# Top-k attention and a two-layer MLP on one core: the second MLP layer as seven block products, with block sums on GpSimd

## The chip, the cores and the metric

The kernel runs on one core of a Trainium2 chip. The metric is the time of one execution on the device, in microseconds (us); lower is better. The time before the change is 1482.96 us, the median of three runs (1481.1 to 1486.69). Engines are named as in the profile: PE is TensorE (matmuls), PEld its weight loads, DVE VectorE, ACT ScalarE, POOL GpSimd, SP the engine that issues most DMAs.

## The reference, cut to what matters

```
scores = (q @ k^T) / sqrt(64)                  # 8 batches x 8 heads, 576 x 576 each
kth    = the 32nd largest score of each row
attn   = softmax of scores, those below kth left out
x      = (attn @ v), heads side by side        # 4608 tokens x 512
h      = x @ w_in                              # 512 x 2048
g      = max(0.01 * h, h)
out    = g @ w_out                             # 2048 x 512
```

All of it is fp32 at the kernel's edges except the weights, which come as 64-bit floats and are rounded on the chip in the first 60 us.

## The kernel before, in words

**Attention.** The work on scores is cut into 144 units of 128 rows for two heads at a time. One step of the main loop starts one unit on DVE and carries the units before it on, so that four or five are in flight: in step s, DVE finds the 32 largest of each row of unit s (`top_k`, L299 to L318: two TENSOR_TENSORs at L306 that sort the halves of a row pairwise, then rounds of MAX8 and MATCH_REPLACE8), POOL makes the bias of unit s-1 (`nbias`, L327 and L328), ACT masks it, takes exponents with their sum and scales it by the reciprocal (`rz`, L344, on DVE; scaling at L347). In the next step POOL splits unit s-2 into two halves (`split`, L356), SP writes these to DRAM and reads them back transposed (L357, L359) into `wT`; two steps later PE weighs the values with it (L398, L410) into `x`, the tokens' input to the MLP. At the end of every even step PE makes the scores of two units (L235) and ACT copies them to SBUF (L242).

**MLP.** Tokens are taken in chunks: two of 128, then seventeen of 256 (`CHUNKS`, L54). For a chunk of 256, the first layer makes the hidden values transposed: for each of 16 blocks of 128 hidden units, four matmuls of 256 columns into `ph` (L467), and after two blocks a Prelu by ACT into `gT` (L473). The second layer takes the 256 tokens as two row tiles; each accumulates 16 matmuls of 512 columns into `pz` (L479), which ACT copies to `o_sb` (L488) and sends to the output by a DMA from its own queue (L489). `ph` and `pz` take turns in two PSUM buffers. The chunks of 128 have a first layer of their own (`hidden_of_few`, L429).

**Order.** The order of the work is written out by hand; nothing reorders it. `mlp` (L455) is a generator that yields the columns of its matmuls as a cost after every few of them. At seven places in a step the main loop calls `mlp_steps(budget)` (L501), which runs it for so many columns; `slot_budget` (L548) spreads the columns that are waiting evenly until the next chunk is due. What is left at the end runs through in one go (L702). Each engine works through its own instructions in order.

**Loads.** Queries and keys of the 32 pairs of heads come by `load_qk` (L162) into five buffers of their own and, for three pairs in eight, into the three `raw` buffers that held the weights at the start; `load_more` (L575, from L592 on for q and k) decides at the end of a step what is loaded next, `load_waiting` (L184) issues one load from a list at the start of a step.

Of the kernel before, what the change touches and what calls it, by code (L numbers as in the profile page):

```python
# [20 lines left out]
def kernel(  # L21
# [23 lines left out]
    HP = DMODEL // P  # L45
# [4 lines left out]
    NFC = DFF // P  # L50
    WCH = 1024
# [2 lines left out]
    CHUNKS = [128] * 2 + [256] * 17  # L54
    assert sum(CHUNKS) == B * S
    CHMAX = max(CHUNKS)
    LOADED, LOADED_V = 5, 5

    const = ctx.enter_context(tc.tile_pool(name="const", bufs=1))
    xpool = ctx.enter_context(tc.tile_pool(name="xpool", bufs=2))  # L60
    loads = ctx.enter_context(tc.tile_pool(name="loads", bufs=LOADED))
    raws = ctx.enter_context(tc.tile_pool(name="raws", bufs=3))
    work = ctx.enter_context(tc.tile_pool(name="work", bufs=2))
# [19 lines left out]
    gT = const.tile([P, NFC, CHMAX], F32, name="gT")  # L83
# [76 lines left out]
    qk_of, v_of = {}, {}  # L160

    def load_qk(pi, at_once=True):  # L162
        if pi % (LOADED + 3) < LOADED:
            qt = loads.tile([P, S], F32, name="qt")
            kt = loads.tile([P, S], F32, name="kt")
        else:
            raw = raws.tile([P, WCH, 4], U16, name="raw").rearrange("p n w -> p (n w)").bitcast(F32)
            qt, kt = raw[:, 0:S], raw[:, S:2 * S]
        waiting.extend([(qt, qT[pi]), (kt, kT[pi])])
        qk_of[pi] = qt, kt  # L170
        if at_once:
            while waiting:
                nc.sync.dma_start(*waiting.pop(0))
# [255 lines left out]
    def hidden_of_few(ch, x):  # L429

        g_of = {}
        for j in range(NFC // 4):
            ph = ps_ml.tile([P, 512], F32, name="ph", tag="ml")
            for c in range(HP):
                nc.tensor.matmul(ph, x[c][:, 0:P], w_in[c][:, j * 512:(j + 1) * 512],  # L435
                                 start=(c == 0), stop=(c == HP - 1))
                if c == 1:
                    yield 2 * 512
            g_of[j] = raws.tile([P, 2 * DMODEL], U16, name="scale", bufs=2).bitcast(F32)
            nc.scalar.activation(g_of[j], ph, AF.Prelu, alpha=SLOPE)  # L440
            yield 2 * 512
            if j:
                yield from turned(j - 1, g_of)
        few[ch] = g_of
# [3 lines left out]
    def turned(j, g_of):  # L448
# [3 lines left out]
        nc.scalar.copy(gT[:, 4 * j:4 * (j + 1), 0:P], pt)  # L452
        yield 2 * P

    def mlp(ch):  # L455

        n = CHUNKS[ch]
        t0 = sum(CHUNKS[:ch])
        x = x_of[ch]
        if ch < EARLY:  # L460
            yield from hidden_of_few(ch, x)
        for f0 in range(0, NFC if ch >= EARLY else 0, 2):
            ph = ps_ml.tile([P, 2, CHMAX], F32, name="ph", tag="ml")
            for i in range(2):
                f = f0 + i
                for c in range(HP):
                    nc.tensor.matmul(  # L467
                        ph[:, i, 0:n], w_in[c][:, f * P:(f + 1) * P], x[c][:, 0:n],
                        start=(c == 0), stop=(c == HP - 1),
                    )  # L470
                    if c == 1 or i == 0 and c == HP - 1:
                        yield 2 * max(n, 225)
            nc.scalar.activation(gT[:, f0:f0 + 2, 0:n], ph[:, :, 0:n], AF.Prelu, alpha=SLOPE)  # L473
            yield 2 * max(n, 225)
        for r0 in range(0, n, P):
            m = min(P, n - r0)
            pz = ps_ml.tile([P, 512], F32, name="pz", tag="ml")
            for f in range(NFC):
                nc.tensor.matmul(  # L479
                    pz[0:m, 0:DMODEL], gT[:, f, r0:r0 + m], w_out[f // 4][:, f % 4, :],  # L480
                    start=(f == 0), stop=(f == NFC - 1),
                )
# [4 lines left out]
            o_sb = work.tile([P, DMODEL], F32, name="o_sb", bufs=1)  # L487
            nc.scalar.copy(o_sb[0:m], pz[0:m, 0:DMODEL])  # L488
            nc.scalar.dma_start(out[t0 + r0:t0 + r0 + m, :], o_sb[0:m])  # L489
# [11 lines left out]
    def mlp_steps(budget):  # L501
        owed[0] += budget
        while owed[0] > 0:
            if running[0] is None:
                if not ready:
                    owed[0] = 0.0
                    return
                running[0] = mlp(ready.pop(0))
            cost = next(running[0], None)
            if cost is None:  # L510
                running[0] = None
            else:
                owed[0] -= cost
                backlog[0] -= cost
# [44 lines left out]
    with tc.manual_schedule():  # L559
# [15 lines left out]
        def load_more(s):  # L575

            at_once = 2
            while len(v_of) < NPAIR:
                n = len(v_of)
                due = values_at(starts[n])[0]  # L580
                if n < LOADED_V:
                    load_v(n)
                elif values_at(last[n - LOADED_V])[0] > s:
                    break
                elif due > s + 2:
                    load_v(n, at_once=False)
                elif at_once:
                    load_v(n)
                    at_once -= 1
                else:  # L590
                    break
            while len(qk_of) < NPAIR:  # L592
                n = len(qk_of)
                if n < LOADED or not to_keep and n < LOADED + 3:
                    load_qk(n)
                elif not to_keep and last[n - LOADED - 3] + 8 <= s and not waiting:
                    load_qk(n, at_once=False)
                else:
                    break

# [36 lines left out]
        def keep(weighed, *place):  # L637
            for u, po in weighed:
                keep_values(u.pairs[0], po, u.b, u.q0)
            attended(*place)  # L640

        for s in range(len(steps) + LAG + 1):
            assert s < 7 or not to_keep
            cur, old, older, new = unit(s), unit(s - 1), unit(s - 2), ()
            in_haste = s - 2 in HASTY
            if s % 2 == 0:
                new = [u for u in steps[s + 2:s + 4] if u]
            if new and new[0] in early_units:
# [24 lines left out]
            if old:  # L673
                exponents(old, 0)
            weighed = values(s, MIDDLE)
            if old:
                exponents(old, 1)
                sums(old)
            keep(weighed, s, MIDDLE)
            mlp_steps(budget)  # L680
            slot()
            if s % 2:
                slot()
            if old:
                reciprocals(old)
            mlp_steps(budget)
            if old:
                normalize(old, 0)
                normalize(old, 1)
            mlp_steps(budget)  # L690
            slot()
            slot()
            if unit(s + 3) in early_units:
                fetch_scores(unit(s + 3))
            mlp_steps(budget)
            if new:
# [5 lines left out]
        mlp_steps(1e9)  # L702


_OUT = ((4608, 512), "float32")
# [56 lines left out]
```

## Time and profile before

| what | us |
|---|---|
| median of three runs | 1482.96 |
| the profiled execution | 1484.13 |
| its span in the trace | 1482.3 |
| PE busy | 1421.1 (96%) |
| DVE busy | 1313.7 (89%) |
| ACT busy | 1035.8 (70%) |
| POOL busy | 504.6 (34%) |
| second layer, L479 | 513.7 busy on PE, 1152 records |
| first layer, L467 | 491.0 busy on PE, 2176 records |

The chain of work that ended last runs 84% through PE, 7% through DVE and 5% through ACT. An fp32 matmul of the code leaves two records each of weight load and matmul, so 1152 records are 576 matmuls. Matmul records overlap each other: a group's busy time divided by its count is shorter than the mean duration of one record. The page cuts the span into 40 slices and gives the busy share of each in tenths. Rows of groups give the line, engine, operation, output and inputs with their shapes and the count, then busy us and mean ns of one, then the idle time before them and what ended it.

### The profile page before, as it was taken

To read this page: it belongs to the slowest core of one execution; us is meant where nothing else is said; L and a number is where in the kernel's file an instruction comes from. 1 tells how busy PE (TensorE), PEld (TensorE's weight loads), DVE (VectorE), ACT (ScalarE), POOL (GpSimd) and SP (SyncE) were. 2 spreads that over 40 slices of the span, in tenths; PEclk is the share of its full clock that TensorE was granted. 3 is DMA by queue.
4 is the path that set the end of the run, shared out by engine and by line. 5 is a ranking of instruction groups with operands and counts; after the bars stand their busy time and mean duration, and the time that the engine had idled before them with its cause. 6 is when DMAs were issued, how large, how long until landed. Compare 5 with 4: busy or idle time off the path is not lost.

```text
span 1482.3 us, 25928 instructions
## 1 busy us (share of the span) xinstructions
PE 1421.1 (96%) x9032; PEld 906.0 (61%) x9034; DVE 1313.7 (89%) x3401; ACT 1035.8 (70%) x2148; POOL 504.6 (34%) x580
## 2 busy tenths in 40 slices
PE   7859989899999999999999999999999999999999
PEld 2335447557575757575766666766666666666674
DVE  7987899899999999999999999999999999999700
ACT  8877777667676767676777777767677777777610
POOL 3211242333433333343333333333433333333400
PEclk9988998999999999999999999999999999999999
DMA  8932152666666654676565655666666555544510
GB/s 335 335 121 96 58 146 68 179 178 167 181 164 174 161 142 129 177 197 186 161 178 161 174 129 142 180 191 176 175 165 173 160 142 129 165 131 140 137 44 15
DMA packets 379252, 232.06 MB, mean 157 GB/s; under 512 B 320368, under 2 KB 321905, under 8 KB 377201
## 3 DMA queue, kind: packets, MB, share of 16 engines
q1 hardware_dynamic: 373936, 220.97, 52.6%
q10 hardware_dynamic: 5184, 9.44, 1.7%
q8 instruction: 71, 1.16, 0.3%
q14 instruction: 61, 0.49, 0.1%
HBM read 55.77 MB, written 95.55 MB: 102 GB/s over the span
## 4 chain that ended last, share of the span: by engine, by line
PE 84%; DVE 7%; ACT 5%; DMA 2%; issue 1%; POOL 1%; SPq 0%; ACTq 0%; DVEq 0%; POOLq 0%
PE pz L479 32%; PE ph L467 31%; PE wide L398 10%; PE wide L235 5%; PE narrow L235 3%; DVE tops L311 2%; DVE pairs L316 1%; PE wide L410 1%; PE ph L435 1%; ACT s_sb L242 1%; ACT s_sb L335 1%; DMA raw<-in_weights_dram 1%; ACT s_sb L332 1%; DVE w_out L156 1%; ACT s_sb L347 1%
## 5 line engine op out<-in xcount | busy, mean ns | idle before, releaser
L311 DVE MAX8 tops<-pairs 128x8 f32<-128x288 f32 (+1 forms) x1152 | 639.0, 596 | 0.0
L479 PE MATMUL pz<-w_out,gT 128*128 128x512 f32 x1152 | 513.7, 599 | 0.5 <-ACT scale L440 0.5
L467 PE MATMUL ph<-x,w_in 128*128 128x256 f32 x2176 | 491.0, 383 | 0.0
L316 DVE MATCH_REPLACE8 pairs<-tops,pairs 128x288 f32<-128x288 f32 (+1 forms) x864 | 461.9, 542 | 0.0
L467 PEld LDWEIGHTS ph<-x,w_in 128*128 128x128 f32 x2176 | 407.8, 190 | 82.3 <-issue 29.6
L327 POOL TENSOR_TENSOR nbias<-tops 128x2 f32<-128x2 f32 x144 | 108.2, 751 | 849.7 <-DVE tops L311 842.3
L479 PEld LDWEIGHTS pz<-w_out,gT 128*128 128x128 f32 x1152 | 215.4, 191 | 258.2 <-issue 255.9
L356 POOL COPY split<-s_sb 128x1152 uint16<-128x1152 uint16 x268 | 298.8, 1142 | 5.1 <-ACT s_sb L347 5.1
L347 ACT ACTIVATE s_sb<-s_sb,rz 128x576 f32<-128x576 f32 x288 | 207.1, 769 | 33.7 <-DVE rz L344 33.3
L335 ACT ACTIVATE s_sb<-s_sb,nbias 128x576 f32<-128x576 f32 x288 | 218.8, 761 | 0.0
L332 ACT ACTIVATE s_sb<-s_sb,nleast 128x576 f32<-128x576 f32 x288 | 208.0, 768 | 4.7
L306 DVE TENSOR_TENSOR pairs<-s_sb 128x576 f32<-128x576 f32 x288 | 205.4, 754 | 4.9
L398 PE MATMUL wide<-wT,vt 128*64 128x128 f32 (+1 forms) x2560 | 158.0, 287 | 12.3 <-ACT wT L375 8.4
L398 PEld LDWEIGHTS wide<-wT,vt 128*64 128x64 f32 (+1 forms) x2560 | 129.4, 140 | 59.2 <-issue 37.7
L242 ACT COPY s_sb<-wide 128x704 f32<-128x704 f32 x130 | 98.4, 757 | 58.1 <-PE wide L235 58.1
L473 ACT ACTIVATE gT<-ph 128x512 f32<-128x512 f32 x136 | 80.5, 592 | 81.5 <-PE ph L467 81.3
L422 ACT COPY x<-wide 128x128 f32<-128x128 f32 (+1 forms) x160 | 32.2, 260 | 136.7 <-PE wide L398 117.5
L488 ACT COPY o_sb<-pz 128x512 f32<-128x512 f32 x36 | 21.1, 587 | 99.1 <-PE pz L479 99.1
L328 POOL TENSOR_SCALAR nbias<-nbias 128x2 f32<-128x2 f32 x144 | 85.8, 596 | 12.6
L344 DVE RECIPROCAL rz<-ze 128x2 f32<-128x2 f32 x144 | 22.4, 156 | 71.7 <-ACT ze L340 71.6
L235 PE MATMUL wide<-kt,qt 64*64 64x352 f32 x704 | 72.8, 473 | 3.8 <-ACT wT L375 3.1
L316 DVE MATCH_VALUE_LOAD pairs<-tops,pairs 128x8 f32 x864 | 65.8, 76 | 0.0
(70 smaller groups left out, 773.3 us busy)
## 6 DMA issues: line engine op xcount, KB each, us to landing
apart<-split SPq DMA_DIRECT2D x268, 288.0 KB, 2.1
raw<-in_weights_dram SPq DMA_DIRECT2D x15, 1024.0 KB, 6.9
vt<-in_vk_dram SPq DMA_DIRECT2D x32, 320.0 KB, 3.5
out_dram<-o_sb ACTq DMA_DIRECT2D x36, 256.0 KB, 2.7
kept<-gT SPq DMA_DIRECT2D x12, 576.0 KB, 3.0
s_sb<-kept SPq DMA_DIRECT2D x12, 576.0 KB, 4.2
qt<-in_qT_dram SPq DMA_DIRECT2D x20, 288.0 KB, 3.5
kt<-in_kT_dram SPq DMA_DIRECT2D x20, 288.0 KB, 3.2
```

The lines of the kernel that those rows point to most:

```text
L235: nc.tensor.matmul(to[r0:r0 + LEFT, i, :], qt[d, q0:q0 + LEFT], kt[d, k0:k1], start=True, stop=True)
L242: nc.scalar.copy(u.both[:, :, k0:k1], to)
L306: nc.vector.tensor_tensor(pairs[:, :, n, :], u.both[:, :, 0:HS], u.both[:, :, HS:S], op)
L311: nc.vector.max(out=u.tops[:, i, r, :], in_=rest[i])
L316: nc.vector.match_replace(out=rest[i], in_to_replace=u.tops[:, i, r, :], in_values=rest[i], imm_value=LOWEST)
L332: nc.scalar.activation(u.s[i], u.s[i], AF.Prelu, bias=u.nleast[:, i:i + 1], scale=1.0, alpha=BELOW)
L335: nc.scalar.activation(u.s[i], u.s[i], AF.Exp, bias=u.nbias[:, i:i + 1], scale=SCALE, accum_out=u.z[:, i:i + 1])
L347: nc.scalar.activation(u.s[i], u.s[i], AF.Copy, bias=0.0, scale=u.rz[:, i:i + 1])
L356: nc.gpsimd.tensor_copy(split, pairs[:, :, h])
L398: nc.tensor.matmul(po[n * D:(n + 1) * D, side, 0:P], v_of[u.pairs[0]][k, at, side, :], u.wT[k, at + side * NKC if at + 1 < NKC else at, :] ...
L467: nc.tensor.matmul(ph[:, i, 0:n], w_in[c][:, f * P:(f + 1) * P], x[c][:, 0:n], start=(c == 0), stop=(c == HP - 1),)
L479: nc.tensor.matmul(pz[0:m, 0:DMODEL], gT[:, f, r0:r0 + m], w_out[f // 4][:, f % 4, :], start=(f == 0), stop=(f == NFC - 1),)
```

## The change

The second layer of the chunks of 256 tokens is done in seven block products in place of eight. The hidden values of a chunk are seen as a 2 x 2 matrix of blocks (two row tiles of 128 tokens, two halves of the 2048 hidden units), `w_out` as 2 x 2 blocks (two halves of the hidden units, two halves of the 512 outputs). Each product is eight matmuls of 256 columns. It needs sums of blocks:

- of the weights, once: `t1`, `t2`, `t4` in the three `raw` buffers, given to POOL from step 7 on, and one block of `w_out` overwritten by a difference when the first chunk of 256 begins;
- of the hidden values, in each chunk: `s1`, `s2`, and two blocks of `gT` overwritten; eight sums of 128 x 512;
- of the products: three sums of 128 x 256 in SBUF. Two partial sums are carried by accumulation in PSUM. ACT copies PSUM out seven times a chunk, 128 x 256 each.

The sums are all POOL's. `sum_later` puts them on a list, `sum_now(3)` issues up to three in the middle of every step, and `sum_now()` the rest at two places in `mlp` where a product is about to need them. The output DMAs of these chunks leave from SP at the start of the next step (`send_now`), four of 128 KB a chunk. The first layer pairs block f0 with block f0 + 8, so that both halves of the hidden values grow together.

Since the `raw` buffers now hold the weights' sums, queries and keys have seven buffers of their own, and their loads are ordered by another condition.

```diff
-    LOADED, LOADED_V = 5, 5
+    LOADED, LOADED_V = 7, 5
...
-        if pi % (LOADED + 3) < LOADED:
-            qt = loads.tile([P, S], F32, name="qt")
-            kt = loads.tile([P, S], F32, name="kt")
-        else:
-            raw = raws.tile([P, WCH, 4], U16, name="raw").rearrange("p n w -> p (n w)").bitcast(F32)
-            qt, kt = raw[:, 0:S], raw[:, S:2 * S]
+        qt = loads.tile([P, S], F32, name="qt")
+        kt = loads.tile([P, S], F32, name="kt")
...
+    def sum_now(count=1000):
+        for to, a, b, op, then in later[:count]:
+            nc.gpsimd.tensor_tensor(to, a, b, op)
+            if then is not None:
+                to_send.append(then)
+        del later[:count]
+
+    def send_now():
+        while to_send:
+            nc.sync.dma_start(*to_send.pop(0))
...
+            sum_later(t1, w_block(0, 1, g), w_block(0, 0, g), ALU.subtract)
+            sum_later(t2, w_block(1, 1, g), t1, ALU.subtract)
+            sum_later(t4, w_block(1, 0, g), t2, ALU.subtract)
...
+            sum_later(w_block(0, 1, g), w_block(1, 1, g), w_block(0, 1, g), ALU.subtract)
...
-            nc.scalar.activation(gT[:, f0:f0 + 2, 0:n], ph[:, :, 0:n], AF.Prelu, alpha=SLOPE)
-            yield 2 * max(n, 225)
+            nc.scalar.activation(halves_of_g[:, :, f0, :], ph, AF.Prelu, alpha=SLOPE)
+            if f0 % 4 == 3:
+                at = slice(f0 - 3, f0 + 1)
+                sum_later(s1[:, at, :], g21[:, at, :], g22[:, at, :], ALU.add)
+                sum_later(s2[:, at, :], s1[:, at, :], g11[:, at, :], ALU.subtract)
+                sum_later(g21[:, at, :], g11[:, at, :], g21[:, at, :], ALU.subtract)
+            yield 2 * n
+
+        def product(to, g, w, first=False):
+            for f in range(HALF):
+                nc.tensor.matmul(to, g[:, f, :], w(f), start=(first and f == 0), stop=(f == HALF - 1),
+                                 skip_group_check=not first)
+                if f % 4 == 3:
+                    yield 4 * COLS
+
+        def keep_sum(ps):
+            part = work.tile([P, COLS], F32, name="o_sb", bufs=6)
+            nc.scalar.copy(part, ps)
+            return part
+
+        def add(part, other, r, j):
+            sum_later(part, part, other, ALU.add, (place(r, j), part))
...
+        pa = ps_ml.tile([P, 512], F32, name="pz", tag="ml")
+        pb = ps_ml.tile([P, 512], F32, name="pz", tag="ml")
+        px, py, pz = pa[:, 0:COLS], pb[:, 0:COLS], pb[:, COLS:2 * COLS]
+        yield from product(px, g11, lambda f: w_at(f, 0), first=True)
+        p1 = keep_sum(px)
+        yield from product(py, g12, lambda f: w_at(f + HALF, 0), first=True)
+        p2 = keep_sum(py)
+        sum_now()
+        for f0 in (0, 4):
+            at = slice(f0, f0 + 4)
+            sum_later(g12[:, at, :], g12[:, at, :], s2[:, at, :], ALU.subtract)
+        yield from product(px, s2, of("t2"))
+        u2 = keep_sum(px)
+        add(p1, p2, 0, 0)
+        yield from product(pz, s1, of("t1"), first=True)
+        p5 = keep_sum(pz)
+        yield from product(px, g21, lambda f: w_at(f, 1))
+        u3 = keep_sum(px)
+        sum_now()
+        yield from product(pz, g12, lambda f: w_at(f + HALF, 1))
+        p35 = keep_sum(pz)
+        add(u3, p5, 1, 1)
+        yield from product(px, g22, of("t4"))
+        c21 = keep_sum(px)
+        add(u2, p35, 0, 1)
+        to_send.append((place(1, 0), c21))
+        yield 0
...
-        return NFC * HP * max(n, 225) + -(-n // P) * NFC * DMODEL
+        return NFC * HP * n + 7 * HALF * COLS
...
-                if n < LOADED or not to_keep and n < LOADED + 3:
+                if n < LOADED:
                     load_qk(n)
-                elif not to_keep and last[n - LOADED - 3] + 8 <= s and not waiting:
-                    load_qk(n, at_once=False)
+                elif last[n - LOADED] // 2 * 2 - 1 <= s and (not waiting or starts[n] <= s + 5):
+                    load_qk(n, at_once=starts[n] <= s + 5)
...
             load_waiting()
+            send_now()
...
             keep(weighed, s, MIDDLE)
+            if s == 7:
+                sum_weights()
+            sum_now(3)
             mlp_steps(budget)
```

The chunks of 128 keep their second layer; only their output leaves in two halves of 256 columns. After the last step, what is left on the two lists is issued.

More of the change, by code (lines that the diff above doesn't have):

```diff
@@ L453, in turned, with w_at, w_block, sum_later @@
         yield 2 * P
+    HALF, COLS = NFC // 2, DMODEL // 2
+    summed = {}
+    def w_at(f, j):
+        return w_out[f // 4][:, f % 4, j * COLS:(j + 1) * COLS]
+    def w_block(i, j, g):
+        return w_out[2 * i + g][:, :, j * COLS:(j + 1) * COLS]
+    later, to_send = [], []
+    def sum_later(to, a, b, op, then=None):
+        later.append((to, a, b, op, then))
+    def sum_now(count=1000):
[7 more added lines that the diff above has]
+            nc.sync.dma_start(*to_send.pop(0))
+    def sum_weights():
+        for name in ("t1", "t2", "t4"):
+            t = raws.tile([P, WCH, 4], U16, name="raw").rearrange("p n w -> p (n w)").bitcast(F32)
+            summed[name] = t.rearrange("p (f n) -> p f n", n=COLS)
+        for g in range(2):
+            t1, t2, t4 = [summed[name][:, 4 * g:4 * (g + 1), :] for name in ("t1", "t2", "t4")]
+            sum_later(t1, w_block(0, 1, g), w_block(0, 0, g), ALU.subtract)
+            sum_later(t2, w_block(1, 1, g), t1, ALU.subtract)
+            sum_later(t4, w_block(1, 0, g), t2, ALU.subtract)
+    def sum_last_weights():
+        for g in range(2):
+            sum_later(w_block(0, 1, g), w_block(1, 1, g), w_block(0, 1, g), ALU.subtract)
     def mlp(ch):
@@ L460, in mlp @@
         if ch < EARLY:
-            yield from hidden_of_few(ch, x)
-        for f0 in range(0, NFC if ch >= EARLY else 0, 2):
+            yield from plain(ch, n, t0, x)
+            return
+        if ch == EARLY:
+            sum_last_weights()
+        halves_of_g = gT.rearrange("p (h f) n -> p h f n", h=2)
+        (g11, g21), (g12, g22) = [[halves_of_g[:, h, :, r * P:(r + 1) * P] for r in range(2)] for h in range(2)]
+        s1 = raws.tile([P, HALF, P], F32, name="top", bufs=2)
+        s2 = raws.tile([P, HALF, P], F32, name="top", bufs=2)
+        for f0 in range(HALF):
             ph = ps_ml.tile([P, 2, CHMAX], F32, name="ph", tag="ml")
             for i in range(2):
-                f = f0 + i
+                f = f0 + i * HALF
                 for c in range(HP):
@@ L471, in mlp @@
                     if c == 1 or i == 0 and c == HP - 1:
-                        yield 2 * max(n, 225)
-            nc.scalar.activation(gT[:, f0:f0 + 2, 0:n], ph[:, :, 0:n], AF.Prelu, alpha=SLOPE)
-            yield 2 * max(n, 225)
+                        yield 2 * n
[5 more added lines that the diff above has]
+                sum_later(g21[:, at, :], g11[:, at, :], g21[:, at, :], ALU.subtract)
@@ new lines, in mlp @@
+            yield 2 * n
+        def product(to, g, w, first=False):
[10 more added lines that the diff above has]
+            sum_later(part, part, other, ALU.add, (place(r, j), part))
@@ new lines, in place, with of @@
+        def place(r, j):
+            return out[t0 + r * P:t0 + (r + 1) * P, j * COLS:(j + 1) * COLS]
+        def of(name):
+            return lambda f: summed[name][:, f, :]
+        pa = ps_ml.tile([P, 512], F32, name="pz", tag="ml")
[4 more added lines that the diff above has]
+        yield from product(py, g12, lambda f: w_at(f + HALF, 0), first=True)
@@ L475, in mlp, with plain @@
+        p35 = keep_sum(pz)
[5 more added lines that the diff above has]
+        yield 0
+    def plain(ch, n, t0, x):
+        yield from hidden_of_few(ch, x)
         for r0 in range(0, n, P):
-            m = min(P, n - r0)
             pz = ps_ml.tile([P, 512], F32, name="pz", tag="ml")
@@ L479, in mlp @@
                 nc.tensor.matmul(
-                    pz[0:m, 0:DMODEL], gT[:, f, r0:r0 + m], w_out[f // 4][:, f % 4, :],
+                    pz[:, 0:DMODEL], gT[:, f, r0:r0 + P], w_out[f // 4][:, f % 4, :],
                     start=(f == 0), stop=(f == NFC - 1),
@@ L486, in mlp @@
                     yield from turned(NFC // 4 - 1, few[ch])
-            o_sb = work.tile([P, DMODEL], F32, name="o_sb", bufs=1)
-            nc.scalar.copy(o_sb[0:m], pz[0:m, 0:DMODEL])
-            nc.scalar.dma_start(out[t0 + r0:t0 + r0 + m, :], o_sb[0:m])
+            for j in range(2):
+                o_sb = work.tile([P, COLS], F32, name="o_sb", bufs=6)
+                nc.scalar.copy(o_sb, pz[:, j * COLS:(j + 1) * COLS])
+                nc.scalar.dma_start(out[t0 + r0:t0 + r0 + P, j * COLS:(j + 1) * COLS], o_sb)
             yield 2 * DMODEL
@@ L702 @@
         mlp_steps(1e9)
+        sum_now()
+        send_now()
 _OUT = ((4608, 512), "float32")
@@ L748 @@
     }
-    nc = _bacc.Bacc("TRN2", target_bir_lowering=False, num_devices=1)
+    nc = _bacc.Bacc("TRN2", target_bir_lowering=False, num_devices=1,
+                     dynamic_dma_scratch_size=1024)
     arrays, args = {}, []
```

## The prediction

> **What bounds the kernel now.** I read the page's busy rows and slices first, then busy time by stretches, the rows by line of the long middle stretch, the waits there, and last the order of time.
>
> ```profile
> PE   7859989899999999999999999999999999999999
> DVE  7987899899999999999999999999999999999700
> ...
> 370.00:1398.00 1028.00, 1027.80 (x6772) 670.23 (x6771) 982.98 (x2576) 738.67 (x1583) 395.53 (x448) 1.00 0.59 162
> 1398.00:1482.30 84.30, 80.75 (x321) 49.06 (x319) 0.17 (x1) 12.71 (x27) 4.83 (x6) 1.00 0.15 44
> ```
>
> The last two rows give start:end, length, then busy time of PE, weight loads, DVE, ACT and POOL, granted clock, DMA share and GB/s. From 370 to 1398 us PE is busy 1027.8 of 1028 us at full clock: work taken from PE there shortens that stretch. But DVE has 983 of the 1028. From 1398 on, DVE has nothing left and PE works alone.
>
> How close DVE is shows in the 112 attention steps of the stretch. A step begins with DVE's two TENSOR_TENSORs (L306). Successive starts:
>
> ```profile
> 902.45 1.43 DVE L306 TENSOR_TENSOR pairs<-s_sb 128x576 f32<-128x576 f32 x2
> ...
> 911.22 1.43 DVE L306 TENSOR_TENSOR pairs<-s_sb 128x576 f32<-128x576 f32 x2
> ...
> 920.92 1.43 DVE L306 TENSOR_TENSOR pairs<-s_sb 128x576 f32<-128x576 f32 x2
> ...
> 929.69 1.43 DVE L306 TENSOR_TENSOR pairs<-s_sb 128x576 f32<-128x576 f32 x2
> ```
>
> Steps take 8.77, 9.70, 8.77. Every even step takes 8.77, which is DVE's own work; the odd ones carry the wait, typically 9.43, 9.81, 10.14 and 9.70 in the four pairs of one chunk. The wait is this one (total us, times, longest):
>
> ```profile
> DVE rz L344 <- ACT ze L340: 41.2, 46, 1.4
> ```
>
> ACT is late there because it copies scores that PE finished late. So DVE's floor is 112 x 8.775 = 982.8 us: DVE can give back at most 45 of the 1028.
>
> **The change, part by part.**
>
> *PE.* Rows of 370 to 1398 (busy us, mean ns); an fp32 matmul of the code shows as two records:
>
> ```profile
> L467 PE MATMUL ph<-x,w_in 128*128 128x256 f32 x1792 | 404.7, 383 | 0.0
> L479 PE MATMUL pz<-w_out,gT 128*128 128x512 f32 x900 | 399.1, 597 | 0.0
> ```
>
> They overlap, so I use busy time by count: 404.7/1792 = 0.2258 us for 256 columns, 399.1/900 = 0.4434 for 512. A chunk's second layer is 32 matmuls of 512 columns, 64 records: 28.38 us. Seven products of 8 matmuls of 256 columns are 112 records: 25.29, with the shape of L467, whose weight load of 0.19 us hides under the 0.2258. That saves 3.09 us a chunk. 900/64 = 14.06 chunks lie in the stretch: **-43.4 us**. It is nearly all that DVE can give back, so PE and DVE end almost level; what DVE loses decides the rest.
>
> *Floor.* The planner spreads a chunk's columns evenly, so each of the 56 pairs of steps loses 0.775 us, all of it in the odd step: 8.66, 9.04, 9.37, 8.93. The first cannot go below 8.775: 0.11 a chunk, **+1.6 us**. In the other three DVE still idles 1.0 us a chunk in all.
>
> *Sums on GpSimd.* A chunk adds eight sums of 512 elements and three of 256. In the changed program they stand after the split copies and before the next step's nbias, and in odd steps only: three, three, three and two of them. POOL has room: the split copies end 3.7 us into the step (914.9 for the step at 911.22) and the next nbias comes with the next step. A sum's duration is not in the trace. Copies of 512 and 1024 elements (0.679, 1.139 us) give 0.22 + 0.0009 an element, so 0.68 us is the low end; 1.14 if two inputs are read one after the other; 2.06 if four-byte inputs also double it. I take 1.14, since POOL's only full-size rows scale with elements. Between dependent POOL operations lies 0.09 us (nbias ends at 1390.04, L328 begins at 1390.13), so three sums are 3.6 us.
>
> Who is queued behind them? nbias and the split copies of the next step, and DVE, if the two disturb each other:
>
> ```profile
> 1389.23 1.43 DVE L306 TENSOR_TENSOR pairs<-s_sb 128x576 f32<-128x576 f32 x2
> 1389.28 0.76 POOL L327 TENSOR_TENSOR nbias<-tops 128x2 f32<-128x2 f32 x1 [5.15 <-DVE tops L311]
> ...
> 1398.05 0.20 POOL L327 TENSOR_TENSOR nbias<-tops 128x2 f32<-128x2 f32 x1 [5.15 <-DVE tops L311]
> ```
>
> The same two-element operation takes 0.76 us when it begins with DVE's TENSOR_TENSOR and 0.20 after the last step, where none follows. It waits for DVE's operation. The split copies beside MAX8 and MATCH_REPLACE8 change nothing (the MAX8 pair takes 0.81 with and without). Whether DVE waits in turn for a long POOL operation the trace hardly shows: L306 spans 0.745 to 0.786 us at most, beside nbias. I assume it does.
>
> The Trainium skill, "SBUF — State Buffer", section "Who interferes with whom", speaks against this change: a VectorE instruction with two SBUF inputs and a GpSimd instruction that reads SBUF exclude each other, and whoever is first holds the port for its whole instruction. If the two shared the port instead, the lock term below would be nothing.
>
> When does a group run? The first two wait for the Prelu of f0 = 3 and f0 = 7, which in ACT's order stand between or just after the masks of the odd step, behind the score copies. In the step at 911.22 the scores end at 914.85; four more matmuls (1.8) or six (2.7) fill ph, and the Prelu takes 0.6: ready about +6.3 and +7.0 us, and with PE 0.775 earlier +5.5 and +6.2. For a sum of d both groups together run 2 x (3d + 0.18) + 5.5 + 6.2 - 2 x 8.775 = 6d - 5.49 us into the next steps: 1.35 us a chunk that DVE's next TENSOR_TENSORs wait. The third and fourth groups wait for nothing late (they start at +3.7 and last 3.2 at most). The idle 1.0 absorbs the larger part: 0.35 x 14 = **+4.9 us**. Ends: at 0.68 nothing waits; at 2.06 it is 6.9, and 0.4 for the third group, net 6.3 x 14 = +88.
>
> The skill's "GPSIMD Engine Reference", section 3.1, gives 4497 ns for a 2048-element fp32 sum; a quarter, an estimate, is 1.12 us, and the term would stay as it is.
>
> *ACT.* Two copies of 0.587 become seven; rows of 128, 448 and 512 columns (0.269, 0.540, 0.592) put 256 columns at 0.38. ACT goes up by 1.5 us a chunk and is 72% busy. What counts is a copy ahead of the exponents of an odd step, where DVE waits for ze: I take one such a chunk, 14 x 0.38 = **+5.3 us**; ends 0 and three, +16.
>
> *Waits of PE.* The products into px wait for the copy of the one before; another product, 16 x 0.2258 = 3.6 us, lies between. The first layer's ph buffers have the same distance now, and no wait of PE for L473 is listed. Product s2 x t2 needs the second group, with 7.2 us of two products and a step's other work between: nothing. Nothing is also the likeliest for SP: the output DMAs moved there stand ahead of the next split's DMAs but wait for sums that ended before that; wT now lands 4.6 us before it is used (1413.1 against 1417.68). With seven buffers for q and k instead of eight places, each reload still precedes its scores by a step, against 3.5 us to landing: nothing, up to +3 at the start, where three pairs are now loaded at once. The weights' eight extra sums are given out once.
>
> *Tail.* Alone, 128 records of 256 columns take 27.79 us and 64 of 512 take 27.63; 112 of 256 are 24.3: -3.3 for the last chunk. The 40 records (17.7 us) of the chunk before lose an eighth less: -2.0. Three output DMAs at the end instead of one: +0.5. **-4.8 us.** One chunk's second layer lies before 370 us, where DVE sets the pace: 0, at best -3.1.
>
> Sum: -43.4 + 1.6 + 4.9 + 5.3 - 4.8 = -36.4. The profiled execution took 1484.13 us (span 1482.3): 1447.7. The median of the runs shown, 1482.96, is 1.2 lower, inside their spread of 1481.1 to 1486.69; I forecast **1448 us**.
>
> **The rivals.**
>
> 1. *Full gain, 1438 us.* DVE doesn't wait for POOL, and the copies find room: only -43.4 + 1.6 - 4.8. For it: when DVE loses time PE gets ahead, scores come earlier and the next sums too. Against: the ze wait is still in every odd step. 0.20.
> 2. *Half of it, 1455 to 1475.* ACT at its end, +16 for 5.3, gives 1458; a sum of 1.3 us instead, (2.31 - 1.0) x 14 = +18 for 4.9, gives 1461; both give 1472. For it: nothing in the trace shows a 256-column copy or a sum. Against: most copies stand where ACT has time. 0.12.
> 3. *No change, 1476 to 1490.* PE waits behind the copies: the score copies, masks and exponents stand in ACT's queue for up to 5.8 us, more than the 3.6 between. One wait of 2.4 us a chunk is 14 x 2.4 = 34, which gives 1482. Against: ph has that risk today and shows no wait. 0.06.
> 4. *Slower, 1531 us.* The port: at 2.06 us a sum the groups run over 3 us into the next step and DVE stands, 1447.7 - 4.9 + 88. Without the lock term the sum is -41.3, so it turns slower when 6d - 5.49 passes 41.3/14 + 1.0 = 3.95 us a chunk, from d = 1.57 us. For it: two-input fp32 is unknown here, and DVE has no slack left. Against: rows per element, and PE's lead as in 1. 0.15.
>
> **How the numbers follow.** My forecast case (1441 to 1455) has 0.47. About 0.5%, 7.4 us, is what a measurement tells from no change. Faster 0.47 + 0.20 + 0.12 = 0.79, within 0.06, slower 0.15. The range goes from rival 1 with the early chunk's 3.1, and 2 for the rounding, to the end of rival 3: 1432 to 1490, leaving out most of rival 4.
>
> **What would show it.** The second layer at 0.226 us a record with 112 a chunk; PE no longer filled from 370 to 1398, the odd steps at 8.8 to 9.4 and the ze wait well below 41 us; POOL sums near 1.14 us; L306 above 0.8 us only after the odd steps of the first two groups. Wrong: L306 with spans of 1.5 us and more in many steps, PE waiting for o_sb copies or for POOL, or even steps above 8.8.

## The result, and the profile after

| | before | after |
|---|---|---|
| median of four runs, us | 1484.83 (1481.1 to 1488.23) | 1465.3 (1463.53 to 1466.58) |
| profiled execution, us | 1484.13 | 1463.53 |
| its span, us | 1482.3 | 1461.8 |
| PE busy, us | 1421.1 | 1373.3 |
| POOL busy, us | 504.6 | 728.6 |

The change made the kernel 1.3% faster: ratio 0.9868, 95% interval 0.9839 to 0.9897. The gain is 19.5 us where 36.4 were worked out. (The forecast's text says 1448 us; its last line has 1445, an earlier value of the sum that I did not carry over.)

First the slices of the changed kernel, and its chain of the work that ended last, by engine:

```profile
PE   7858988789999999999999999999899999999998
DVE  7987899999999999999999999999899999999700
...
PE 65%; DVE 18%; DMA 7%; ACT 6%; issue 2%; POOL 2%; SPq 0%; ACTq 0%; DVEq 0%; POOLq 0%
```

The lines of the changed kernel have other numbers: L302 is the pairwise sort (L306 before), L340 is `rz` (L344), L394 and L406 weigh the values (L398 and L410), L353 and L355 are the split's write and the transposing DMA (L357 and L359), L526 is the second layer (L479).

PE's share of the chain fell from 84% to 65%, DMA's rose from 2% to 7% and DVE's from 7% to 18%. To see where, I compare the same work in both traces: the 111 DVE steps from step 32 to the last, counted from one `nbias` to the next. Busy time of the changed kernel in these steps and in the rest (columns as before: PE, weight loads, DVE, ACT, POOL, clock, DMA share, GB/s):

```profile
378.24:1380.70 1002.46, 982.58 (x7381) 796.74 (x7380) 978.47 (x2553) 751.39 (x1640) 561.08 (x598) 1.00 0.61 164
1380.70:1461.80 81.10, 75.49 (x403) 65.06 (x401) 0.17 (x1) 15.35 (x37) 21.59 (x22) 1.00 0.16 47
```

PE, which was filled to 1027.8 of 1028 us, now idles 20 us here. The waits in that stretch (total us, times, longest):

```profile
DVE rz L340 <- ACT ze L336: 19.6, 14, 4.2
PE wide L394 <- DMA wT<-apart: 14.8, 8, 4.4
PE wide L406 <- DMA vt<-in_vk_dram: 3.4, 3, 1.6
```

DVE's wait for `ze` fell from 41.2 us in 46 waits of at most 1.4 to 19.6 in 14 waits of up to 4.2: fewer and longer. The other two are new: PE's wait for `wT` was 0.2 us before, and for `vt` there was none. Together PE now waits 18.2 us for DMAs at the weighing of the values (L394, L406).

The balance by spans. Before step 32: 378.51 to 378.24 us, -0.3. The 111 steps: 1019.5 to 1002.5, -17.0. The tail: 84.2 to 81.1, -3.1. Together -20.4 of 1482.3 - 1461.8 = 20.5. DVE's floor for the steps is 111 x 8.775 = 974.0; what lies over it, which I call the **excess**, went from 45.5 to 28.5 us.

The groups of the second layer in the changed kernel, and its sums (min/median/max ns):

```profile
L526 PE MATMUL pz<-w_out,gT 128*128 128x256 f32 x1088 | 245.2, 381 | 0.6 <-ACT o_sb L533 0.6
L526 PE MATMUL pz<-raw,top 128*128 128x256 f32 x544 | 125.0, 384 | 0.0
L526 PE MATMUL pz<-raw,gT 128*128 128x256 f32 x272 | 62.0, 381 | 0.0
```

```profile
L467 POOL TENSOR_TENSOR top<-gT x34: 1265/1278/1291, 260.3 to 1434.0; 128x512 f32<-128x512 f32 x34
```

432.2 us for 1904 records is 0.227 us each, as worked out (0.226). PE waits 0.6 us for the copies and not at all for POOL. A sum takes 1.28 us, not 1.14.

Counted by chunks of eight steps, there are two kinds. A plain chunk fell from 74.18 us to 71.0: steps of 8.77, 8.78, 9.09, 8.78, 8.77, 8.79, 9.30, 8.72, and a gain of 3.2 us, more than the 2.26 that -43.4 + 1.6 + 4.9 + 5.3 gives for each of 14 chunks. But some chunks hold one or two steps of 10 to 13 us: 11.71 in the chunk at 378 us, 11.05, 11.59, 13.09, 11.12 in later ones. This is the place of the longest, in order of time (start, us, engine, line; in brackets the wait before it). L302 marks the start of a step:

```profile
1030.00 0.53 SPq L293 DMA_DIRECT2D s_sb<-kept  x1
...
1030.57 0.43 SPq L182 DMA_DIRECT2D kt<-in_kT_dram  x1
...
1031.51 1.43 SPq L353 DMA_DIRECT2D apart<-split  x2
...
1037.25 2.60 SPq L355 DMA_TRANSPOSE wT<-apart  x1
1037.67 1.43 DVE L302 TENSOR_TENSOR pairs<-s_sb 128x576 f32<-128x576 f32 x2
...
1041.92 3.81 PE L394 MATMUL wide<-wT,vt 128*64 128x128 f32 x38 [4.40 <-DMA wT<-apart]
...
1045.82 0.43 ACT L418 COPY x<-wide 128x128 f32<-128x128 f32 x2 [4.44 <-PE wide L394]
...
1058.03 0.17 DVE L340 RECIPROCAL rz<-ze 128x2 f32<-128x2 f32 x1 [4.22 <-ACT ze L336]
```

The same place in a plain chunk of the same kernel:

```profile
814.43 1.42 SPq L353 DMA_DIRECT2D apart<-split  x2
...
817.67 2.37 SPq L355 DMA_TRANSPOSE wT<-apart  x1
...
820.59 1.43 DVE L302 TENSOR_TENSOR pairs<-s_sb 128x576 f32<-128x576 f32 x2
...
822.30 2.35 PE L394 MATMUL wide<-wT,vt 128*64 128x128 f32 x40
```

And in a plain chunk of the kernel before:

```profile
898.53 2.35 SPq L359 DMA_TRANSPOSE wT<-apart  x1
...
902.45 1.43 DVE L306 TENSOR_TENSOR pairs<-s_sb 128x576 f32<-128x576 f32 x2
...
906.77 2.35 PE L398 MATMUL wide<-wT,vt 128*64 128x128 f32 x40
```

In both places of the changed kernel, PE weighs the values 4.6 us after the transposing DMA is issued, which is about when `wT` lands; in the kernel before it came 8.2 us after the issue. Two things differ between the long step and the plain one. The transpose was issued 5.7 us after the split's write instead of 3.2; a fetch of kept scores (576 KB, L293) and a load of keys (288 KB) had been issued just ahead of that write. And PE was earlier: it makes no scores here, since those of these units were kept, and began the weighing (its first two records, at 1037.09) 0.6 us ahead of the step's start, against 1.7 after it in the plain chunk and 4.3 after it in the kernel before. PE stands 4.4 us, ACT with it, and 16 us later DVE waits 4.2 for `ze`. PE gained time and arrives before its data.

### The profile page after: what moved, and what is told of

Its sections match the earlier page's. It is cut to its first block, busy times and chain, and to the rows that moved or that the text cites. A ratio compares the mean times of both kernels' runs of the same rounds, so it can differ in the third digit from the quotient of the medians.

```text
span 1461.8 us, 27967 instructions
## 1 busy us (share of the span) xinstructions
PE 1373.3 (94%) x9848; PEld 1065.6 (73%) x9850; DVE 1317.9 (90%) x3401; ACT 1058.5 (72%) x2235; POOL 728.6 (50%) x775
## 4 chain that ended last, share of the span: by engine, by line
PE 65%; DVE 18%; DMA 7%; ACT 6%; issue 2%; POOL 2%; SPq 0%; ACTq 0%; DVEq 0%; POOLq 0%
PE ph L510 23%; PE pz L526 22%; PE wide L394 9%; DVE tops L307 8%; DVE pairs L312 6%; PE wide L231 4%; DMA wT<-apart 4%; PE narrow L231 2%; PE pz L578 2%; DVE pairs L302 2%; DMA apart<-split 2%; ACT s_sb L238 1%; PE ph L431 1%; DMA vt<-in_vk_dram 1%; ACT s_sb L331 1%
## 5 line engine op out<-in xcount | busy, mean ns | idle before, releaser
L526 PE MATMUL pz<-w_out,gT 128*128 128x256 f32 x1088 | 245.2, 381 | 0.6 <-ACT o_sb L533 0.6
L526 PEld LDWEIGHTS pz<-w_out,gT 128*128 128x128 f32 x1088 | 205.7, 190 | 31.5 <-issue 2.5
L328 ACT ACTIVATE s_sb<-s_sb,nleast 128x576 f32<-128x576 f32 x288 | 214.4, 770 | 4.7
L302 DVE TENSOR_TENSOR pairs<-s_sb 128x576 f32<-128x576 f32 x288 | 212.3, 778 | 5.0
L394 PE MATMUL wide<-wT,vt 128*64 128x128 f32 (+1 forms) x2560 | 165.4, 290 | 30.2 <-DMA wT<-apart 21.5
L394 PEld LDWEIGHTS wide<-wT,vt 128*64 128x64 f32 (+1 forms) x2560 | 134.6, 141 | 68.1 <-issue 31.3
L526 PE MATMUL pz<-raw,top 128*128 128x256 f32 x544 | 125.0, 384 | 0.0
L526 PEld LDWEIGHTS pz<-raw,top 128*128 128x128 f32 x544 | 101.1, 190 | 21.2 <-issue 8.4
L231 PE MATMUL wide<-kt,qt 64*64 64x352 f32 x1040 | 105.0, 474 | 3.6 <-ACT wT L371 2.9
L533 ACT COPY o_sb<-pz 128x256 f32<-128x256 f32 x119 | 43.8, 368 | 57.1 <-PE pz L526 57.1
```

The costliest lines, as they stand in the source:

```text
L231: nc.tensor.matmul(to[r0:r0 + LEFT, i, :], qt[d, q0:q0 + LEFT], kt[d, k0:k1], start=True, stop=True)
L302: nc.vector.tensor_tensor(pairs[:, :, n, :], u.both[:, :, 0:HS], u.both[:, :, HS:S], op)
L328: nc.scalar.activation(u.s[i], u.s[i], AF.Prelu, bias=u.nleast[:, i:i + 1], scale=1.0, alpha=BELOW)
L394: nc.tensor.matmul(po[n * D:(n + 1) * D, side, 0:P], v_of[u.pairs[0]][k, at, side, :], u.wT[k, at + side * NKC if at + 1 < NKC else at, :] ...
L526: nc.tensor.matmul(to, g[:, f, :], w(f), start=(first and f == 0), stop=(f == HALF - 1), skip_group_check=not first)
```

## The experiments

**Theory 1**: PE, now early, stands at the weighing for a late `wT`, and hands the wait on to DVE through the scores, ACT and `ze`. **Theory 2**: the sums cost the time by the port that GpSimd and DVE share. **Theory 3**: SP's order does it, the loads and output DMAs in front of the split's. Excess and waits below are those of the 111 steps. Each kernel is the changed one with the edit shown, where nothing else is said.

### The weighing moved later

```diff
-            weighed = values(s, MIDDLE)
...
-            keep(weighed, s, MIDDLE)
...
                 normalize(old, 1)
+            keep(values(s, MIDDLE), s, MIDDLE)
```

> Edit: PE's weighing of the values and ACT's copies of x move from the middle of the step to behind the scaling of the unit. Theory 1 (late values: PE, now ahead, reaches the weighing before wT has landed, stands 18 us in all, and the next scores, ze and rz are late): the waits of PE for wT and vt go, DVE's wait for ze falls from 19.6 to under 6 us, time 1448 to 1455. Theory 2 (the port: DVE and the split copies stand behind GpSimd's sums): the sums are where they were, 1462 to 1467. Theory 3 (SP: loads and output DMAs ahead of the transposes make wT late): the lateness stays but hurts less, 1453 to 1462.

Measured: **1436.94 us** (1432.74 to 1440.89), ratio to before 0.9689 (0.9651 to 0.9727). The excess fell from 28.5 to 12.8, step 32 begins 5.7 us earlier, the tail is 2.2 shorter: 23.6 us in the spans. The waits:

```profile
PE wide L394 <- DMA wT<-apart: 5.0, 4, 2.1
DVE rz L340 <- ACT ze L336: 4.7, 6, 2.3
PE wide L406 <- DMA vt<-in_vk_dram: 1.7, 1, 1.7
```

The same work in another place takes 15.7 us off the long stretch, and a plain chunk is hardly shorter for it (70.9 us). That is theory 1. The time is below the 1448 to 1455 expected; 7.8 of the 23.6 us lie ahead of step 32 and in the tail. This version beats both kernels.

The same edit on the kernel **before**:

> The kernel before with the weighing and the copies behind the scaling. Theory 1: PE was behind there and wT had 4 us of cover, so little is won, 1474 to 1484, the part before 370 us. If the edit is good in itself and has nothing to do with the change: 1455 to 1465.

Measured: 1471.58 us, 0.9918 (0.9892 to 0.9945). Nearly all of it lies ahead of step 32, which begins at 367.04 instead of 378.51; the excess stays (44.5 against 45.5). So later weighing does almost nothing for the long stretch while PE is late there anyway. With the weighing late in both, the change is worth 1471.6 - 1436.9 = 34.7 us, close to the 36.4 worked out (31.6 between the spans of the profiled executions).

Only ACT's copies of `x` moved behind the scaling, PE's weighing left where it was:

```diff
-            keep(weighed, s, MIDDLE)
...
                 normalize(old, 1)
+            keep(weighed, s, MIDDLE)
```

> The changed kernel with only ACT's copies of x behind the scaling; PE still weighs the values in the middle of the step. If a late wT hurts because the copies hold up the scaling and so the next split: most of the gain of the edit of both, 1437 to 1446. If it hurts because PE stands at the weighing: 1455 to 1466.

Measured: 1467.71 us, 0.9895 (0.9867 to 0.9923); excess 33.7, PE's wait for `wT` 17.1. No gain: it is PE that must not stand there, not ACT's order.

### The sums and the port

No sums on GpSimd at all:

```diff
-        later.append((to, a, b, op, then))
+        if then is not None:
+            to_send.append(then)
```

> Leaves out all sums on GpSimd: the products read blocks as they are, and partial sums are sent unadded. PE, ACT and the DMAs do the same work. Theory 1: only the 7 us that L302 lost are won, 1456 to 1460, and PE still waits for wT some 15 us. Theory 2: the long steps go as well, 1440 to 1449. Theory 3: as theory 1.

Measured: 1473.0 us, 0.9923 (0.9896 to 0.9949), slower than with the sums. The longest L302 is back at 0.786 us, so no sum held it up; the excess is 41.9.

```profile
DVE rz L340 <- ACT ze L336: 40.0, 19, 6.7
PE wide L394 <- DMA wT<-apart: 22.4, 9, 5.6
```

This refutes theory 2 as the cause of the shortfall, and missed my number as well: the waits of theory 1 grew. Why they grow without the sums I did not find.

No sums, and the weighing late:

> Leaves out all sums on GpSimd (products read blocks as they are, partial sums go out unadded), with the weighing and copies behind the scaling. Theory 1: with the lateness gone the sums cost what L302 loses, 1427 to 1433, where with the weighing early leaving them out made it slower. If leaving them out is bad in itself: 1445 or more.

Measured: 1436.84 us, 0.9684 (0.9656 to 0.9713); excess 12.9. With the weighing late the sums make no difference (1436.94 with them), so my 1427 to 1433 was too low, but this also speaks against the sums as the cause.

Sums held to the next step unless they were listed before the step began, so that none runs into DVE's TENSOR_TENSORs; weighing in the middle, and then late:

```diff
-            sum_now(3)
+            sum_now(min(3, sum(at < s for at in given_at)))
```

> The changed kernel with sums held to the next step unless they were listed when the step began, the weighing in the middle of the step. If the port were what is lost: 7 us less, 1455 to 1459. Theory 1: DVE's freed time only lets the late wT show more, as without sums, 1464 to 1474.

Measured: 1467.89 us, 0.9899 (0.9881 to 0.9917); no L302 above 0.785 us, PE's wait for `wT` 16.6, excess 31.4. Taking the collisions away gives nothing back.

> The changed kernel with the weighing and copies behind the scaling, and with sums held to the next step unless they were on the list when the step began, so that none begins late in a step. If one group in each chunk holds up DVE by 0.53 us through the port: 14 x 0.53 = 7 us below the edit of the weighing alone, 1427 to 1433, no L302 above 0.8 us. If the 0.53 comes from elsewhere: 1435 to 1440.

Measured: 1438.98 us, 0.9693 (0.9667 to 0.9719), excess 13.6. A plain chunk still takes 70.9: the 0.53 us that L302 lost in a chunk return as `ze` waits in the odd step (12.1 us in all for 4.7). My number was too low because it added up two gains of which PE allows only one: 70.9 us is PE's time for a chunk, and DVE's is 8 x 8.775 = 70.2. PE is indeed busy for all of the 70.89 us of a plain chunk: in the one from 513.98 us here, and in the one from 514.89 with the weighing alone moved.

The first two sums of each group issued twice, weighing late:

```diff
             nc.gpsimd.tensor_tensor(to, a, b, op)
+            if again:
+                nc.gpsimd.tensor_tensor(to, a, b, op)
```

> The weighing behind the scaling as before, and s1 and s2 each summed twice with the same result, so that the first two groups of a chunk are five sums of 1.28 us instead of three. If DVE stands behind a sum that is running (and nbias and the split behind the group): the two groups run some 2.5 and 3 us into the next steps, up to 5 us a chunk, 1480 to 1507. If DVE is not held: 1436 to 1442.

Measured: 1462.65 us, 0.987 (0.9841 to 0.9899): 25.7 us slower than the same kernel with single sums. A plain chunk takes 72.6 us, with steps of 10.63 and 10.77 after the two groups. The line of L302 in this kernel and, under it, in the changed one:

```profile
L302 DVE TENSOR_TENSOR pairs<-s_sb x288: 743/757/1835, 60.9 to 1373.3; 128x576 f32<-128x576 f32 x144
```

```profile
L302 DVE TENSOR_TENSOR pairs<-s_sb x288: 743/753/1291, 60.7 to 1372.6; 128x576 f32<-128x576 f32 x144
```

So DVE does stand behind GpSimd (0.75 us becomes up to 1.84; L302 is busy 244.4 us in all, against 211.6 with single sums and late weighing), and longer groups are paid for, though less than I expected. At one sum of 1.28 us they are not. One such meeting in the changed kernel:

```profile
1018.99 1.28 POOL L467 TENSOR_TENSOR gT<-gT 128x512 f32<-128x512 f32 x1
1019.66 1.89 DVE L302 TENSOR_TENSOR pairs<-s_sb 128x576 f32<-128x576 f32 x2
```

### What makes wT late

Loads and output DMAs behind the transpose instead of ahead of the split's write:

```diff
-            load_waiting()
-            send_now()
             if old:
                 limits(old)
             if older and not in_haste:
                 transpose(older)
+            load_waiting()
+            send_now()
```

> Edit: the loads and output DMAs that SP issues at the start of a step go behind the split's DMAs and the transpose. Theory 1: a part of the lateness at most, 1459 to 1466. Theory 2: no change, 1463 to 1467. Theory 3: the waits of PE for wT go, 1446 to 1454.

Measured: 1477.84 us, 0.9963 (0.9946 to 0.9981); excess 40.3, PE's wait for `wT` 16.9. Worse, which no theory expected: with the loads no longer ahead of the split's write, the waits are as long.

Output DMAs issued from ACT's queue:

```diff
-            nc.sync.dma_start(*to_send.pop(0))
+            nc.scalar.dma_start(*to_send.pop(0))
```

> The changed kernel with its output DMAs issued by ACT instead of SP, at the same place. If the output DMAs ahead of the split's on SP make wT late: PE's waits for wT shrink, 1450 to 1458. If they have no part in it: 1462 to 1470, ACT paying some 0.1 us for each.

Measured: 1475.53 us, 0.9953 (0.9934 to 0.9972); wait for `wT` 19.4. Worse too: that the four output DMAs stand on SP is not the cause. These two speak against theory 3 as an order on the queue.

The kernel **before** with seven buffers for queries and keys and the new order of loads (and with the argument `dynamic_dma_scratch_size=1024` of the program's constructor, which the changed kernel also has):

> The kernel before with the changed loads alone: seven buffers for q and k and the new conditions. Theories 1 and 2: PE is behind there and wT has 4 us of cover, so 1482 to 1488, as before. Theory 3: waits of PE for wT appear, 1489 or more.

Measured: 1486.36 us, 1.0008 (0.9986 to 1.003). The new loads by themselves cost nothing while PE is late.

Three kernels then leave traffic out, so that they do not compute the reference's result. No reloads of q, k and v:

```diff
     def load_qk(pi, at_once=True):
+        if pi >= LOADED:
+            qk_of[pi] = qk_of[pi - LOADED]
+            return
```

> The changed kernel without the reloads: from the eighth pair of heads on, q and k are those of seven pairs before, from the sixth on v is that of five before, so nothing of them is fetched. If the loads beside the split's DMAs are what makes wT late in the long steps: PE's waits for wT and vt shrink from 18 to under 5 us, only the steps after a fetch of kept scores stay long, 1445 to 1454. If wT is late without them (the way through split, two DMAs and a transpose is simply as long as a step): 1460 to 1466.

Measured: 1457.9 us, 0.9833 (0.9812 to 0.9854); excess 25.8, wait for `wT` 14.3 (15.2 over a window some us longer, as the next expectations have it), for `vt` none. Between the two expectations.

No fetches of kept scores:

```diff
-        nc.sync.dma_start(u.both.rearrange("p i n -> p (i n)"), kept_of[u])
+        nc.gpsimd.memset(u.both.rearrange("p i n -> p (i n)"), 0.0)
```

> The changed kernel, but the twelve fetches of kept scores (576 KB each, from step 26 on) are left out: those twelve units get zeros from a GpSimd memset instead. In the changed kernel PE waits 14.8 us for wT between 378 and 1381 us; the steps with the waits of 2.87, 1.13, 2.31, 1.86 and 4.40 us (12.6 together) have a fetch issued within the 6 us ahead of the split's DMAs, three others only a reload of keys or none. Theory a (the DMA traffic issued just ahead of the split makes wT land late, and PE, now early, stands for it): PE's wait for wT falls to 2 to 5 us, rz's wait for ze from 19.6 to 6 to 10, and the time to 1450 to 1456 us. Theory b (PE simply runs ahead until something stops it, so that a wait taken away at one place comes back at another): the waits stay at 12 or more and the time at 1460 to 1467.

Measured: 1455.08 us, 0.98 (0.9771 to 0.9829); excess 20.4, wait for `wT` 9.4. The time is that of theory a; the waits are not: `wT` fell to 9.4 where 2 to 5 were expected, and `rz`'s wait for `ze` to 11.7 where 6 to 10 were.

Neither:

> The changed kernel without the twelve fetches (zeros from a GpSimd memset) and without the reloads of queries and keys from the eighth pair of heads and of values from the sixth on (earlier buffers are used again): of the DMAs only split, transposes and outputs are left in the middle. Without the reloads alone it took 1457.9 us, with 15.2 us of PE's wait for wT and 20.9 of rz's for ze. Theory a (traffic ahead of the split makes wT late): PE's wait for wT is under 2 us, rz's for ze under 4, the 111 steps lose 8 to 12 us over the floor where they lost 25.8, and the time is 1440 to 1446 us. Theory b (PE runs ahead until something stops it): the waits stay at 10 or more, and the time at 1453 to 1460.

Measured: 1446.24 us, 0.975 (0.9727 to 0.9773); excess 14.7. (L400 and L346 are L394 and L340 here.)

```profile
PE wide L400 <- DMA wT<-apart: 7.4, 6, 1.9
DVE rz L346 <- ACT ze L342: 7.0, 11, 1.7
```

The fetches take 8.1 us of the excess with them, the reloads 2.7, both 13.8, and what is left is within 2 us of the kernel with late weighing (12.8). So the traffic of these loads makes up about half of the excess. Theory a does not hold whole: the time and the excess lie a little outside its ranges, the waits midway between theory a's and theory b's. 7.4 us of the wait, at most 1.9 each, stay without any of these loads, and all six of these waits are in steps where the transpose was issued 3.2 us after the write, as in a plain step: there PE arrives when `wT` lands although nothing delays it. In the changed kernel three of the eight waits, 3.9 of 14.8 us, are of this kind.

How the loads delay `wT` is not shown. That they stand ahead of the write cannot be all of it: with the loads issued behind the transpose the waits were no shorter. And they are not the only delay: the transpose was issued more than 4.5 us after the write in 30 of the 111 steps of the changed kernel (at most 5.9 us), but also in 20 with no loads at all (at most 5.2).

## Why the prediction was right and wrong

The direction and the size of PE's saving were right; the gain was half of what was forecast, in the main for one reason.

**The step that failed** is "Nothing is also the likeliest for SP ... wT now lands 4.6 us before it is used (1413.1 against 1417.68)", and with it the price of nothing for PE's waits. The row that was read, and the landing times of this DMA in the trace of before (us from issue, median):

```profile
1410.72 2.38 SPq L359 DMA_TRANSPOSE wT<-apart  x1
...
1417.68 2.35 PE L398 MATMUL wide<-wT,vt 128*64 128x128 f32 x40
```

```profile
wT<-apart SPq DMA_TRANSPOSE x134, 4.5
```

1413.1 is 1410.72 + 2.38, the end of SP's issue, and not the landing. By its semaphore this transpose landed at 1415.1, so the cover was 2.6 us. (The 4 us of cover in two of the expectations is too much as well.) That is less than the 3.1 us a chunk that the change takes from PE, the engine that waits there. Nor does one step stand for all: over the 55 weighings between step 32 and the last, PE began a median of 2.3 us after the landing of the transpose issued in the step before, and at worst 0.6 us ahead of it. In the changed kernel the median is 0.8 us after, and the worst 4.8 us ahead: that is the step with the wait of 4.4, which comes after the first two records (0.43 us). Now every delay of the DMA counts: 18.2 us of new waits, and moving the weighing later gained 15.7 us in the stretch, where the change by itself had gained 17.0. The landing and the spread of the cover could be read in the trace of before.

The other terms:

- *PE, -43.4.* The price of a record was right (0.227 for 0.226), and plain chunks gained 3.2 to 3.3 us for the 3.09. But five chunks, those with two units whose scores were made at the start, took 71.9 to 72.9 us before, 361.5 together, and cannot go below DVE's 70.2; with late weighing they take 355.2. They gained 6.3 for the 15.5 counted. I had taken all chunks as the plain one that I read.
- *The lock, +4.9, and ACT's copies, +5.3.* Neither was paid. The sums take 1.28 us (for 1.14) and a copy 0.368 (for 0.38); the sums lengthen L302 by some 0.5 us a chunk, 6.9 in all (212.3 us busy for 205.4), where 1.35 a chunk were worked out. But a plain chunk is 70.9 us with and without the sums: PE is busy throughout and still its bound, 0.7 above DVE's floor, so that DVE has idle time for the longer L302. The 10.2 us of costs that were not paid and the 9 us of gain that the five chunks could not give cancel. So the sum for the stretch, -31.6, agrees with the kernel that has no large wait at the weighing (-32.7, 45.5 to 12.8) partly by luck.
- *Floor, +1.6.* Right in kind: two of the four odd steps fell to 8.78, the others to 9.09 and 9.30 (worked out: 8.775, 9.04, 9.37 and 8.93).
- *Tail, -4.8.* It gave -3.1. The loads at the start and the early chunk, counted as nothing, gave -0.3.
- *The rivals.* The measured time lies in the range of rival 2, but not by its causes: ACT's copies and longer sums cost nothing in a plain chunk, which PE fills. Rival 4's mechanism exists, and the doubled sums show its price; with d = 1.28 us the point from which it decides (1.57 by my working) was not reached. Rival 3's wait of PE was the right kind at the wrong place: for a DMA, not for a copy.

Left open: how the loads delay `wT`, why the kernels without sums, with later loads and with output DMAs from ACT have more of the `wT` waits than the changed kernel, and what gives the weighing's move its gain ahead of step 32, 5.7 us here and 11.5 in the kernel before.

## What to carry to other kernels

Work taken from the engine that bounds a kernel also takes away the cover of every DMA that this engine never waited for: for each of its inputs, compare the landing (not the end of the issue) with the arrival as it will be after the change, over many steps of the loop, with those among them in which that engine has least to do or the DMAs most. If a wait of that kind appears, look for work that can go ahead of it in the engine's order before shortening the DMA: here an edit of three lines gave back 15.7 us in the long stretch. And when a loop has steps of several lengths, price the change in each kind of chunk, since an engine close behind (DVE at 70.2 us against 70.9) caps the gain in the short ones.

## What the runs showed of the hardware

- A GpSimd sum of two fp32 inputs took 1.278 us for 512 elements and 0.729 for 256: 0.18 us and 2.15 ns an element. By this line 1024 elements, as in the sums of the weights, would be 2.38 us; these took 2.36 to 2.38. The Trainium skill's "GPSIMD Engine Reference", section 3.1, has 4497 ns for 2048; by these two it would be 4.57 us, an estimate, so the page and the runs agree. My quarter of it was too short because it left out most of the fixed 0.18.
- GpSimd and DVE hold each other up, in both directions. Before, `nbias` took 0.76 us where it began with DVE's TENSOR_TENSOR and 0.20 where none followed; here a sum that began at 1018.99 and lasted 1.28 us stretched the pair of L302 that began at 1019.66 to 1.89 us (1.43 otherwise), and doubled sums stretched one instruction to 1.84. This is the exclusion that "SBUF — State Buffer", "Who interferes with whom", of the Trainium skill describes; over a chunk it took some 0.5 us.
- The transposing DMA of `wT` landed 4.5 us after its issue (median before; 4.2 to 6.2), while its row on the issuing queue lasts only some 2.4 us.
- The way from the split's write to the issue of its transpose took 3.2 us in a plain step and 5.7 in one with 864 KB issued just ahead, on a core whose DMA share over the stretch is 0.61; with no loads at all it was still up to 5.2.
